# Two groups' transposes moved from TensorE to the DMA, and one pair of scores moved into the next tile, in a fused retention and feed-forward kernel

## The chip, the cores and the metric

The kernel runs on one core of a Trainium2 chip. The metric is the device time of one execution in microseconds (us); one profiled execution gives the trace. The span in the profile (first to last instruction) is about 2 us shorter than the device time. An execution of this one-core program is labelled slow when it is over 1.5% above the fastest of the same kernel; the text says where slow ones are quoted, and ratios use fast ones alone. The chip was not the same in every set of rounds (the record numbers them: e1 to e4 chip 2, f1 to f4 chip 1, h0 to h2 chip 6, i1 chip 5), so times are compared within a set.

## The reference

Eight batches of eight heads do retention (attention without softmax, with a decay by distance), and the result goes through a feed-forward layer whose nonlinearity is h·cos(h).

```python
scores = (1/sqrt(64)) * q @ k.T                  # q, k, v: (8, 8, 576, 64)
Dmat   = where(rel >= 0, gamma[h] ** rel, 0.0)   # rel = i - j
attn   = (scores * Dmat) @ v
x      = attn.transpose(0, 2, 1, 3).reshape(4608, 512)
h      = x @ w_in                                # (512, 2048)
out    = (h * cos(h)) @ w_out                    # (2048, 512), float32 out
```

## The kernel before

The 4608 tokens are 36 groups of 128. Each group's q and k are scaled (POOL), rounded to bf16 into `qks`, and transposed into `qkT`. Then come its scores (`sc`), its share of a running state (`st`) and its attention output (`ov`), which DVE or ACT copies into `xT`. Tiles of tokens (512, 256, 256, then seven of 512) go through `h = x @ w_in` (`mm1`, source line L275) and `o = g @ w_out` (`mm2`, L292). The small products of later groups are put between the products of `mm2` by a list `todo`: the number is the index of the `mm2` product in front of which the work goes. In words the first tile is tile n = 0, so "the fifth tile" is n = 4.

```python
widths = [512, 256, 256] + [512] * 7
N_PE_T = 8                       # groups below this are transposed on PE

def transposes(g, banks=None, only=(0, 1)):
    qks, vb, qkT, qT = tiles["a", g]
    if g >= N_PE_T:
        nc.sync.dma_start(qkT, qks.rearrange("s m h d -> s (m h d)"), transpose=True)
        return
    for m in only:               # 4 PE transposes and one ACT copy, for q and for k
        ...

def feed(s):                     # after output block s: issue loads and DMA transposes on SP
    while True:
        while prepared < min(loaded, NG, 2 * s + 7, s + 11):
            prep(prepared); prepared += 1
            ...
        if N_PE_T <= transposed < min(prepared, s + 11) and (
            transposed <= loaded - 2 or loaded == NG
        ):
            transposes(transposed); transposed += 1
        elif loaded < min(NG, 2 * s + 8, s + 13):
            load(loaded); loaded += 1
        else: break
...
elif n == 1:
    todo = [(4, lambda: transposes(6, "mb")), (9, lambda: transposes(7, "mb"))]
    todo += pair(6, "ab", 16, 27)
elif n == 2:
    todo = pair(g, "ab", 11, 25, "m")
    todo += [(25, lambda: scores2(g + 2)), (29, lambda: state(g + 2))]
    ...
```

All loads of q, k and v, output stores and DMA transposes are issued in program order by one engine, SP. A transpose late in that queue is late for its scores.

Of the kernel before, what the change touches and what calls it, by code (L numbers as in the profile page):

```python
# [17 lines left out]
def kernel(  # L18
# [16 lines left out]
    nc = tc.nc  # L35
# [8 lines left out]
    NG = NTOK // P  # L44
# [8 lines left out]
    widths = [512, 256, 256] + [512] * 7  # L53
    assert sum(widths) == NTOK
    starts = [sum(widths[:n]) for n in range(len(widths))]
    N_PE_T = 8

    consts = ctx.enter_context(tc.tile_pool(name="consts", bufs=1))
    first = ctx.enter_context(tc.tile_pool(name="first", bufs=1))
# [87 lines left out]
# [5 lines that stand above are left out]
        for m in only:  # L152
            ps = psum.tile([P, HG, P], BF16, tag=banks[m], name="tr")
            for hg in range(HG):
                nc.tensor.transpose(  # L155
                    ps[:, hg, :],
                    qks[:, m, 2 * hg : 2 * hg + 2, :].rearrange("s h d -> s (h d)"),
                    ident,
                )
            nc.scalar.copy(qkT[:, m * HG : (m + 1) * HG, :], ps)  # L160
        if ("fv", g) in tiles and g != 3:
            nc.scalar.copy(vb, tiles.pop(("fv", g)))
# [60 lines left out]
    def attn_out(gs, bank, evac=nc.vector.tensor_copy):  # L223


        ps = psum.tile([P, len(gs), HG, P], F32, tag=bank, name="ov")
        for x, g in enumerate(gs):
            c = g % PER
            if c == 0:
                continue  # L230
            qT = tiles["a", g][3]
            sb = tiles.pop(("sb", g))
            n = HP if c == MIX else P
            for hg in range(HG):
                nc.tensor.matmul(  # L235
                    ps[:, x, hg, :n],
                    lhsT=sb[:, hg, :],
                    rhs=qT[:, hg, :n],
                    start=(hg == 0),
                    stop=False,  # L240
                    skip_group_check=True,
                )
        for x, g in enumerate(gs):
            vb = tiles["a", g][1]
            ret = tiles.pop(("ret", g))
            for hg in range(HG):
                for he in range(2):
                    nc.tensor.matmul(  # L248
                        ps[he * D : he * D + D, x, hg, :],
                        lhsT=vb[:, 2 * hg + he, :],  # L250
                        rhs=ret[:, he, hg, :],
                        start=(g % PER == 0 and hg == 0),
                        stop=(hg == HG - 1),
                        skip_group_check=True,
                    )
        n = max(m for m in range(len(starts)) if starts[m] <= gs[0] * P)
        if ("x", n) not in tiles:
            tiles["x", n] = xp.tile([P, DG, 512], BF16, tag="xT", name="xT")
        t0 = gs[0] * P - starts[n]
        evac(  # L260
            tiles["x", n][:, :, t0 : t0 + len(gs) * P].rearrange("p c (x i) -> p x c i", i=P), ps
        )
# [45 lines left out]
    def feed(s):  # L308

        nonlocal loaded, prepared, transposed  # L310
        while True:
            while prepared < min(loaded, NG, 2 * s + 7, s + 11):
                prep(prepared)
                prepared += 1
                if transposed < N_PE_T:
                    transposed += 1

            if N_PE_T <= transposed < min(prepared, s + 11) and (
                transposed <= loaded - 2 or loaded == NG
# [114 lines left out]
    def pair(g, banks, sc, av, out=None):  # L434

        mid = (sc + av) // 2
        return [
            (sc - 5, lambda: state(g)),
            (sc, lambda: (scores(g, banks[0]), scores(g + 1, banks[1]))),
            (mid, lambda: state(g + 1)),  # L440
            (av, lambda: attn_out([g, g + 1], out or banks[0])),
        ]

    def scores2(g):
        if g < NG:
            scores(g, "a")
            scores(g + 1, "b")

    late = []
    for n, w in enumerate(widths):  # L450

        if n in (0, 3):
            halves = [(h, et) for et in range(0, ET, 4) for h in range(2)]
            if n == 3:
                halves.sort()
            blocks = [(et, half * 256, 256) for half, et in halves]
        elif n == 1:
            blocks = [(et, half * P, P) for half in range(2) for et in (0, 8)]
        else:
            blocks = [(et, 0, w) for et in range(0, ET, 1024 // w)]  # L460
        banks = {0: "abmabmab", 1: "bmba", 2: "bmab", 3: "mamabmab"}.get(n, "abmabmab")
        for i, (et, c0, cw) in enumerate(blocks):

            inside = {
                (0, 0): {2: lambda: (attn_out([3], "n"), state(3))},
                (1, 0): {4: lambda: scores(5, "a")},
                (1, 1): {3: lambda: attn_out([5], "a", evac=nc.scalar.copy)},
            }.get((n, i), {})
            mm1(n, et, c0, cw, banks[i], inside)
            if (n, i) == (3, 1):  # L470
                late.pop()()

        g = starts[n] // P + w // P
        if n == 0:
            todo = [
                (45, lambda: transposes(4, "ab")),
                (49, lambda: state(4)),
                (50, lambda: scores(4, "a")),
                (57, lambda: attn_out([4], "a")),
                (61, lambda: transposes(5, "ba")),  # L480
                (63, lambda: state(5)),
            ]
        elif n == 1:
            todo = [(4, lambda: transposes(6, "mb")), (9, lambda: transposes(7, "mb"))]
            todo += pair(6, "ab", 16, 27)
        elif n == 2:
            todo = pair(g, "ab", 11, 25, "m")
            todo += [(25, lambda: scores2(g + 2)), (29, lambda: state(g + 2))]
            late += [lambda: (state(g + 3), attn_out([g + 2, g + 3], "b"))]
        elif n + 1 < len(widths):  # L490
            todo = [
                (5, lambda: state(g)),
                (12, lambda: scores2(g)) if n == 3 else (0, lambda: None),
                (
                    25 if n == 3 else 20,
                    lambda: (
                        attn_out(
                            [g, g + 1], "m", nc.scalar.copy if n == 3 else nc.vector.tensor_copy
                        ),
                        scores2(g + 2),  # L500
                    ),
                ),
                (16, lambda: state(g + 1)),
                (36, lambda: state(g + 2)),
                (52, lambda: (attn_out([g + 2, g + 3], "m"), scores2(g + 4))),
                (45, lambda: state(g + 3)),
            ]
        else:
            todo = []
        todo.sort(key=lambda u: u[0])  # L510
        order, cols = [], [(0, DM)]
        for tsi in range(w // P):
            if (n + 1, tsi + 1) == (len(widths), w // P):
                cols = [(0, DM // 2), (DM // 2, 3 * DM // 4), (3 * DM // 4, DM)]
            order += [(tsi, et, c0, c1) for c0, c1 in cols for et in range(ET)]
        if n == 0:

            part = 3 * ET // 4
            order[: 2 * ET] = [
                (tsi, et, 0, DM)  # L520
                for tsi, et in [(t, e) for e in range(part) for t in range(2)]
                + [(t, e) for t in range(2) for e in range(part, ET)]
            ]
        for i, (tsi, et, c0, c1) in enumerate(order):
            while todo and todo[0][0] <= i:
                todo.pop(0)[1]()
            mm2(n, tsi, et, c0, c1)
        assert not todo
# [30 lines left out]
```

## Time and profile before

| | before |
|---|---|
| device time, median of the first 3 executions | 308.35 us (308.3 to 310.02) |
| span in the profile | 306.3 us |
| PE busy | 300.5 us (98%) |
| DVE, ACT, POOL busy | 57%, 38%, 32% |
| granted TensorE clock | 1.000 |

Lines of the page of the kernel before: span, busy time by engine, the span in 40 slices (7.66 us each; a digit is the busy share in tenths, PEclk the granted clock), and the chain of waits that ended last.

```profile
span 306.3 us, 5685 instructions
...
PE 300.5 (98%) x2361; PEld 171.2 (56%) x2361; DVE 175.8 (57%) x180; ACT 117.2 (38%) x136; POOL 99.0 (32%) x123
...
PE   7899999999999999999999999999999999999996
...
DMA  8999999999999999999993999189925300010012
...
PE 94%; SPq 2%; DMA 2%; DVE 0%; POOL 0%; issue 0%; ACT 0%; ACTq 0%
```

PE is the limit: after the first slices it is nearly never idle, and it is 94% of the chain. The DMA row is also 9 for the first half of the span: the SP queue runs behind its work there, and only what it delivers just in time matters.

PE's instructions of the kernel before in order of time. Columns: start us, duration, engine, line, operation, out<-in, shape, count, and in brackets idle time in front of it. A merged row's duration includes the last product's modelled end, so what counts is the distance between two starts.

```profile
58.33 0.61 PE L155 MATMUL tr<-ident,qks 128*128 128x128 bf16 x8
58.78 1.24 PE L292 MATMUL o<-w_out_sb,gT 128*128 128x512 bf16 x5
59.86 0.61 PE L155 MATMUL tr<-ident,qks 128*128 128x128 bf16 x8
60.30 0.59 PE L292 MATMUL o<-w_out_sb,gT 128*128 128x512 bf16 x2
...
60.96 1.24 PE L292 MATMUL o<-w_out_sb,gT 128*128 128x512 bf16 x5
...
66.41 1.25 PE L292 MATMUL o<-w_out_sb,gT 128*128 128x512 bf16 x5
67.79 7.15 PE L275 MATMUL h<-xT,w_in_sb 128*128 128x256 bf16 x64
...
81.94 0.62 PE L177 MATMUL sc<-qkT 64*128 64x128 bf16 x16
...
115.01 0.62 PE L177 MATMUL sc<-qkT 64*128 64x128 bf16 x16
```

Each lot of 8 transposes takes 0.45 us until the next product starts (58.33 to 58.78, 59.86 to 60.30). The five products at 66.41 need 5 × 0.216 = 1.08 us, so PE is free at 67.49, and the third tile's first product starts at 67.79: the hole of 0.3 us. The last row is the pair of scores (groups 16 and 17) that the change moves.

The SP queue of the kernel before, at group 8's and group 11's transposes (columns as above; the duration is the time that SP is held by the issue).

```profile
47.50 1.40 SPq L109 DMA_DIRECT2D fv<-in_v_dram  x1
49.00 1.05 SPq L303 DMA_DIRECT2D out_dram<-ot  x1
...
56.60 3.01 SPq L150 DMA_TRANSPOSE qkT<-qks  x1
...
74.17 2.02 SPq L150 DMA_TRANSPOSE qkT<-qks  x1
```

Group 11's transpose lands 5.0 us after its issue began, at 79.2 us. The 16 score products at 81.94 us are groups 10 and 11; group 11's half starts 0.28 us later, at 82.2, with 3.0 us of room.

### The profile page before, as it was taken

What the parts mean: (1) busy time and instruction counts of PE and PEld (TensorE: products, weight loads), DVE (VectorE), ACT (ScalarE), POOL (GpSimd) and SP (SyncE); (2) the same over time, 40 slices, a digit from 0 to 9 for tenths busy, and PEclk for the clock granted to TensorE, in tenths of its full rate; (3) what the DMA queues carried; (4) which work ended last, traced back from release to release, by engine and by line L of the source; (5) the groups of instructions that cost most, each with busy time, mean ns of one, the idle gap of its engine ahead of it and who ended that gap; (6) DMA issues with size and microseconds to landing.
All of it is one profiled execution on the core that took longest, in us unless ns stands there. A gap on an engine that the chain in (4) does not pass through costs nothing.

```text
span 306.3 us, 5685 instructions
## 1 busy us (share of the span) xinstructions
PE 300.5 (98%) x2361; PEld 171.2 (56%) x2361; DVE 175.8 (57%) x180; ACT 117.2 (38%) x136; POOL 99.0 (32%) x123
## 2 busy tenths in 40 slices
PE   7899999999999999999999999999999999999996
PEld 3478547757588554454545554455445544554444
DVE  5776425565777746656576556755676547624610
ACT  3566234715046223631264026411651165105611
POOL 2740066634554534544533334314430000000000
PEclk9999999999999999999999999999999999999999
DMA  8999999999999999999993999189925300010012
GB/s 210 213 211 206 205 230 229 190 198 246 164 243 208 196 253 199 268 220 205 258 205 58 223 218 225 23 190 208 243 48 77 99 35 0 36 68 34 2 68 69
DMA packets 148697, 49.65 MB, mean 162 GB/s; under 512 B 138688, under 2 KB 144192, under 8 KB 148672
## 3 DMA queue, kind: packets, MB, share of 16 engines
q1 hardware_dynamic: 144448, 45.10, 78.5%
q0 software_dynamic: 4224, 4.19, 8.2%
q8 instruction: 18, 0.29, 0.4%
q14 instruction: 7, 0.06, 0.1%
HBM read 36.70 MB, written 9.44 MB: 151 GB/s over the span
## 4 chain that ended last, share of the span: by engine, by line
PE 94%; SPq 2%; DMA 2%; DVE 0%; POOL 0%; issue 0%; ACT 0%; ACTq 0%
PE h L275 41%; PE o L292 41%; PE ov L248 3%; PE sc L177 3%; PE st L206 2%; PE ov L235 2%; DMA fk<-in_k_dram 2%; SPq L109 2%; PE tr L155 1%; PE sc L168 0%; DVE xT L260 0%; POOL qks L135 0%; SPq L336 0%; ACT ot L301 0%; ACTq L301 0%
## 5 line engine op out<-in xcount | busy, mean ns | idle before, releaser
L292 PE MATMUL o<-w_out_sb,gT 128*128 128x512 bf16 (+2 forms) x608 | 134.4, 369 | 0.0
L275 PE MATMUL h<-xT,w_in_sb 128*128 128x512 bf16 (+2 forms) x832 | 127.5, 314 | 0.1
L284 DVE TENSOR_TENSOR gT<-h,cosh 128x1024 bf16<-128x1024 f32 x72 | 88.2, 1225 | 55.9 <-ACT cosh L283 55.8
L275 PEld LDWEIGHTS <-w_in_sb 128*128 128x128 bf16 x832 | 75.8, 98 | 50.4 <-issue 0.4
L283 ACT ACTIVATE cosh<-h,half_pi 128x1024 f32<-128x1024 f32 x72 | 80.2, 1113 | 52.0 <-PE h L275 52.0
L292 PEld LDWEIGHTS <-gT 128*128 128x128 bf16 x608 | 55.3, 98 | 56.2
L134 POOL TENSOR_TENSOR qks<-fq,gq 128x512 bf16<-128x512 f32 x32 | 33.3, 1042 | 104.3 <-DMA fq<-in_q_dram 102.0
L301 ACT COPY ot<-o 128x512 f32<-128x512 f32 (+2 forms) x38 | 21.4, 563 | 115.4 <-PE o L292 115.4
L135 POOL TENSOR_TENSOR qks<-fk,gk 128x512 bf16<-128x512 f32 x35 | 36.5, 1042 | 13.1 <-DMA fk<-in_k_dram 11.4
L186 DVE TENSOR_TENSOR ret<-sc,tri 128x1024 bf16<-128x1024 f32 x32 | 38.0, 1218 | 4.6 <-PE sc L177 4.5
L215 DVE TENSOR_TENSOR sb<-st,diag_105 128x512 bf16<-128x512 f32 x32 | 22.0, 687 | 27.8 <-PE st L206 27.8
L260 DVE CAST xT<-ov 128x1024 bf16<-128x1024 f32 (+1 forms) x16 | 18.5, 1158 | 23.5 <-PE ov L248 23.5
L141 POOL CAST vb<-fv 128x512 bf16<-128x512 f32 x32 | 19.5, 610 | 7.7 <-DMA fv<-in_v_dram 5.7
L206 PEld LDWEIGHTS <-qks 128*128 128x128 bf16 (+1 forms) x128 | 9.5, 98 | 7.0 <-issue 0.4
L248 PE MATMUL ov<-ret,vb 128*64 128x128 bf16 x288 | 12.1, 223 | 0.0
L206 PE MATMUL st<-vb,qks 128*128 128x128 bf16 (+1 forms) x116 | 11.2, 220 | 0.1
L177 PEld LDWEIGHTS <-qkT 64*128 64x128 bf16 x288 | 8.1, 94 | 5.0 <-ACT qkT L160 2.3
L235 PEld LDWEIGHTS <-sb 128*128 128x128 bf16 x128 | 8.3, 98 | 3.8
L160 ACT COPY qkT<-tr 128x512 bf16<-128x512 bf16 x12 | 6.6, 588 | 9.3 <-PE tr L155 9.3
L177 PE MATMUL sc<-qkT 64*128 64x128 bf16 x256 | 10.1, 218 | 0.0
L248 PEld LDWEIGHTS <-vb 128*64 128x64 bf16 x288 | 8.7, 109 | 2.0
L235 PE MATMUL ov<-qkT,sb 128*128 128x128 bf16 (+1 forms) x116 | 8.8, 216 | 0.0
(49 smaller groups left out, 57.3 us busy)
## 6 DMA issues: line engine op xcount, KB each, us to landing
out_dram<-ot SPq DMA_DIRECT2D x35, 256.0 KB, 3.1
fk<-in_k_dram SPq DMA_DIRECT2D x32, 256.0 KB, 4.8
fv<-in_v_dram SPq DMA_DIRECT2D x32, 256.0 KB, 4.9
fq<-in_q_dram SPq DMA_DIRECT2D x28, 256.0 KB, 4.1
w_in_sb<-in_moe_w_in_dram POOLq DMA_DIRECT2D x4, 512.0 KB, 8.7
w_out_sb<-in_moe_w_out_dram POOLq DMA_DIRECT2D x4, 512.0 KB, 15.9
fq_111<-in_q_dram SPq DMA_DIRECT2D x2, 512.0 KB, 4.4
fq<-in_q_dram SPq DMA_DIRECT2D x8, 128.0 KB, 3.8
```

The costliest lines, as they stand in the source:

```text
L134: nc.gpsimd.tensor_tensor(out=qks[:, 0], in0=fq, in1=tq, op=ALU.mult)
L135: (nc.vector if g == 3 else nc.gpsimd).tensor_tensor(out=qks[:, 1], in0=fk, in1=tk, op=ALU.mult)
L177: nc.tensor.matmul(ps[:, he, hg, :], lhsT=qkT[d0 : d0 + D, HG + hg, :], rhs=qT[d0 : d0 + D, hg, :], start=True, stop=True,)
L186: nc.vector.tensor_tensor(out=ret.rearrange("p a b i -> p (a b) i"), in0=ps.rearrange("p a b i -> p (a b) i"), in1=mask.unsqueeze(1).to_br ...
L206: nc.tensor.matmul(ps[:, hg, :], lhsT=qks[p0:, 1, 2 * hg : 2 * hg + 2, :].rearrange("s h d -> s (h d)"), rhs=vs[p0:, 2 * hg : 2 * hg + 2, ...
L215: nc.vector.tensor_tensor(out=sb, in0=ps, in1=diag2.unsqueeze(1).to_broadcast([P, HG, P]), op=ALU.mult,)
L235: nc.tensor.matmul(ps[:, x, hg, :n], lhsT=sb[:, hg, :], rhs=qT[:, hg, :n], start=(hg == 0), stop=False, skip_group_check=True,)
L248: nc.tensor.matmul(ps[he * D : he * D + D, x, hg, :], lhsT=vb[:, 2 * hg + he, :], rhs=ret[:, he, hg, :], start=(g % PER == 0 and hg == 0), ...
L275: nc.tensor.matmul(ps[:, j, :], lhsT=w_in_sb[:, dg, (et + j) * P : (et + j + 1) * P], rhs=xT[:, dg, c0 : c0 + w], start=(dg == 0), stop=(d ...
L283: nc.scalar.activation(cosh, ps, ACTF.Sin, bias=half_pi, scale=1.0)
L284: nc.vector.tensor_mul(gT[:, et : et + m, c0 : c0 + w], ps, cosh)
L292: nc.tensor.matmul(ps, lhsT=gT[:, et, tsi * P : (tsi + 1) * P], rhs=w_out_sb[:, et, c0:c1], start=(et == 0), stop=(et == ET - 1),)
```

## The change

The intent is to take 16 transposes off PE, the limiting engine. Two more transposes in the DMA queue make every later one land later; group 17's was the tightest of those, so its scores, at the end of the fourth tile, move into the fifth. With them the fifth tile's first attention output goes from index 20 to 25, and its copy from DVE to ACT.

```diff
-    N_PE_T = 8
+    N_PE_T = 6
...
         elif n == 1:
-            todo = [(4, lambda: transposes(6, "mb")), (9, lambda: transposes(7, "mb"))]
-            todo += pair(6, "ab", 16, 27)
+            todo = pair(6, "ab", 16, 27)
...
-                (12, lambda: scores2(g)) if n == 3 else (0, lambda: None),
+                (12, lambda: scores2(g)) if n in (3, 4) else (0, lambda: None),
                 (
-                    25 if n == 3 else 20,
+                    25 if n in (3, 4) else 20,
                     lambda: (
-                        attn_out([g, g + 1], "m", nc.scalar.copy if n == 3 else ...),
+                        attn_out([g, g + 1], "m", nc.scalar.copy if n in (3, 4) else ...),
                         scores2(g + 2),
...
-                (52, lambda: (attn_out([g + 2, g + 3], "m"), scores2(g + 4))),
+                (
+                    52,
+                    lambda: (attn_out([g + 2, g + 3], "m"), scores2(g + 4 if n > 3 else NG)),
+                ),
```

## The prediction

> **What bounds the kernel now.** TensorE. The page's first part gives PE 300.5 of 306.3 us (98%) at full granted clock; the chain of waits is 94% PE, 41% each in the two big products. In order of time PE idles about 6 us, nearly all before 20 us; after that I find one hole, 0.3 us at 67.5 us, ended by DVE's xT copy. So only PE time removed, or PE waits added, count. ACT (38%), DVE (57%) and POOL (32%) have slack. The DMA is the second limit: its row is nearly always 9 until about 160 us, and the SP queue runs late there: the output that ACT copied at 49.2 us is issued at 70.9 us.
>
> **What the change removes.** Sixteen PE transposes. In PE's order of time two lots of 8 start at 58.33 and 59.86 us, each followed 0.45 us later by the next product: 0.9 us, all on the critical path. Four ACT copies of 0.59 us go too; with ACT's slack they are worth nothing.
>
> **What it adds.** Two DMA transposes on SP, one behind the loads of group 7 (about 49 us), one behind those of group 8 (about 55 us). Transposes issued there take SP 2.0 to 3.0 us and land 4.6 to 6.0 us after their issue begins. The Trainium skill, "Advanced Engine Details and Errata", section "X-Bar Transpose (TRN2)", says such transposes are as fast as regular DMAs; here a group's three loads take about 3.6 us of queue and an output 0.9, so the 17.6 us from group 8's transpose to group 11's leave about 1.7 us each (estimate), against a load's 1.2. So everything later in the queue moves by 3.4 us, less 0.4 to 1.2 us that SP now waits for POOL at group 8: 2.2 to 3 us, kept until the backlog ends near 159 us.
>
> **Who feels it.** Landing against use, before: group 11 lands at 79.2, its scores start at 82.2 (3.0 us spare, 2.1 once PE is 0.9 earlier); group 15: 101.9 against 107.3; group 17: 113.4 against 115.3, which would stall. That last the second part cures: those scores go to 12 products into the fifth tile, about 134 us. This follows the fourth tile's working pattern and adds no PE work. Group 7 should land near 60 us, its scores come at 61.5: just in time. Expected stalls, lost on PE: 0 to 0.9 us at group 11, 0 to 0.5 us at groups 6 and 7.
>
> **Prediction.** Gain 0.9 us, less about 0.3 expected stall: 307.7 us against 308.35. Range for 8 in 10: 307.0 to 308.7. Faster by over 2%: 0.01; within 2%: 0.98; slower by over 2%: 0.01.
>
> **What would show each step.** (a) No PE transposes after 50 us; the product at 60.96 us starts near 60.06. (b) Thirty DMA transposes, not 28; group 11's is issued 2 to 3 us later than 74.17. (c) The scores of groups 10 and 11 near 81.1 us, with a hole of 0 to 1 us before group 11's, ended by the DMA of qkT. (d) The fifth tile's first scores near 134 us, without a hole; later PE times early by the net gain. (e) The DMA's busy stretch ends 2 to 3 us later.
>
> **What would make it wrong.** A transpose that costs the full queue much more than 1.7 us: then groups 7, 11 and 15 stall and the change loses up to 2 us. A shift swallowed by holes in the DMA: then the whole 0.9 us is gained. New DVE or bank waits in the fifth tile.

## The result, and the profile after

The changed kernel took 307.93 us (median of 6 executions, 307.82 to 308.19), the kernel before 308.33 us (6 executions, 308.22 to 310.02). The ratio is 0.9979, with a 95% interval from 0.9958 to 1.0: the same within 2%, and about 0.4 us less. The interval reaches 1.0, so these times alone do not prove the gain; it is read from the traces below. (A ratio here is the mean time of one kernel's fast runs over that of the other's of the same rounds, so it is not quite the ratio of the medians.)

The page of the changed kernel.

```profile
span 305.9 us, 5619 instructions
...
PE 297.5 (97%) x2311; PEld 170.8 (56%) x2345; DVE 174.7 (57%) x179; ACT 116.1 (38%) x133; POOL 99.1 (32%) x123
...
PE 93%; SPq 2%; DMA 2%; issue 1%; DVE 0%; POOL 0%; ACT 0%; ACTq 0%
```

PE busy must not be read as a gain of 3 us: this trace misses some matmul records (582 instead of 608 of the `o` products), seen below as gaps of 0.16 us put down to "issue". Start times are the safer measure.

PE of the changed kernel in order of time, at the same places as before.

```profile
57.72 2.32 PE L292 MATMUL o<-w_out_sb,gT 128*128 128x512 bf16 x10
...
60.10 1.24 PE L292 MATMUL o<-w_out_sb,gT 128*128 128x512 bf16 x5
...
65.55 1.25 PE L292 MATMUL o<-w_out_sb,gT 128*128 128x512 bf16 x5
66.93 7.15 PE L275 MATMUL h<-xT,w_in_sb 128*128 128x256 bf16 x64
...
81.08 0.62 PE L177 MATMUL sc<-qkT 64*128 64x128 bf16 x16
...
131.87 1.67 PE L292 MATMUL o<-w_out_sb,gT 128*128 128x512 bf16 x7
133.47 0.62 PE L177 MATMUL sc<-qkT 64*128 64x128 bf16 x16
```

The transposes are gone. Every landmark up to 116 us is 0.86 us earlier: 60.96 to 60.10, 67.79 to 66.93, 81.94 to 81.08. No hole stands in front of group 11's scores. The hole at the third tile is still there (65.55 + 1.08 = 66.63, then 66.93). The moved scores are at 133.47; the seven products in front of them end at 131.87 + 7 × 0.216 = 133.38, so 0.09 us is lost between them.

The SP queue of the changed kernel.

```profile
48.02 1.34 SPq L109 DMA_DIRECT2D fv<-in_v_dram  x1
49.46 2.10 SPq L150 DMA_TRANSPOSE qkT<-qks  x1
...
54.56 3.10 SPq L150 DMA_TRANSPOSE qkT<-qks  x1
...
59.94 2.27 SPq L150 DMA_TRANSPOSE qkT<-qks  x1
...
75.94 2.05 SPq L150 DMA_TRANSPOSE qkT<-qks  x1
```

The rows are groups 6, 7, 8 and 11. Group 8's transpose is issued 3.34 us later than before (56.60 to 59.94). Group 11's transpose is issued 1.77 us later (74.17 to 75.94) and lands 5.2 us after that, at 81.14. Its scores start at 81.08 + 0.28 = 81.36. It made it by 0.2 us.

The end of both kernels: ACT's last copy of an output, in ACT's order of time, then SP's wait for output DMAs at the very end, in the table of waits (total us, times, longest us). First the kernel before, ACT and SP:

```profile
303.56 0.27 ACT L301 COPY ot<-o 128x128 f32<-128x128 f32 x1 [0.63 <-PE o L292]
```

```profile
SPq L554 <- DMA out_dram<-ot: 0.7, 1, 0.7
```

Then the changed kernel, ACT and SP:

```profile
302.81 0.27 ACT L301 COPY ot<-o 128x128 f32<-128x128 f32 x1 [0.63 <-PE o L292]
```

```profile
SPq L556 <- DMA out_dram<-ot: 1.1, 2, 0.8
```

PE's work, whose end ACT's last copy marks, finishes 0.75 us earlier (303.56 to 302.81), but the span is only 0.38 us shorter (306.33 to 305.95). The tail from the start of that copy to the end went from 2.77 to 3.14 us. The records of SP's wait instructions show why. At the end SP checks all DMA semaphores, in a fixed order, about 0.06 us per instruction (column 1: when the instruction started, us; then the semaphores it waits for):

```
before: last output issued at 303.86 on semaphore 118    changed: issued at 303.10 on semaphore 103
304.24  117, 116                                         303.48  117, 116
304.30  101, 115                                         303.83  101, 115
304.37  103, 114                                         304.68  103, 114   <- the last output has landed
304.44  104, 113                                         304.75  104, 113
304.50  105, 112                                         304.81  105, 112
304.56  106, 111                                         304.87  106, 111
304.62  108, 110                                         304.93  108, 110
304.68  109, 100                                         304.99  109, 100
305.43  118, 107   <- the last output has landed         305.05  118, 107
```

SP's DMAs take eight semaphores in turn (101, 103, 104, 105, 106, 108, 109, 118). Before, the last output happened to have the one that is checked last, so all the other checks were done while it was under way. Two more DMAs on SP turn this by two places: now it has the one checked third, and six checks come behind the landing: 305.05 − 304.68 = 0.37 us. So the account is: 0.86 us off PE, 0.11 back at the moved scores, 0.37 back in the tail, 0.38 us net.

### The profile page after: what moved, and what is told of

Its sections match the earlier page's. It is cut to its first block, busy times and chain, and to the rows that moved or that the text cites. A ratio compares the mean times of both kernels' runs of the same rounds, so it can differ in the third digit from the quotient of the medians.

```text
span 305.9 us, 5619 instructions
## 1 busy us (share of the span) xinstructions
PE 297.5 (97%) x2311; PEld 170.8 (56%) x2345; DVE 174.7 (57%) x179; ACT 116.1 (38%) x133; POOL 99.1 (32%) x123
## 4 chain that ended last, share of the span: by engine, by line
PE 93%; SPq 2%; DMA 2%; issue 1%; DVE 0%; POOL 0%; ACT 0%; ACTq 0%
PE h L275 41%; PE o L292 40%; PE ov L248 3%; PE sc L177 3%; PE ov L235 2%; PE st L206 2%; DMA fk<-in_k_dram 2%; SPq L109 2%; PE tr L155 0%; PE sc L168 0%; DVE xT L260 0%; POOL qks L135 0%; SPq L336 0%; ACT ot L301 0%; ACTq L301 0%
## 5 line engine op out<-in xcount | busy, mean ns | idle before, releaser
L292 PE MATMUL o<-w_out_sb,gT 128*128 128x512 bf16 (+2 forms) x582 | 130.3, 367 | 2.3 <-issue 1.6
L260 DVE CAST xT<-ov 128x1024 bf16<-128x1024 f32 (+1 forms) x15 | 17.3, 1153 | 20.9 <-PE ov L248 20.9
L160 ACT COPY qkT<-tr 128x512 bf16<-128x512 bf16 x8 | 4.5, 587 | 8.0 <-PE tr L155 8.0
```

What stands on the lines that cost most here:

```text
L292: nc.tensor.matmul(ps, lhsT=gT[:, et, tsi * P : (tsi + 1) * P], rhs=w_out_sb[:, et, c0:c1], start=(et == 0), stop=(et == ET - 1),)
```

## The experiments

Theory: the gain is PE's 0.86 us; the second part of the change is needed because group 17's transpose would otherwise come late, and costs 0.1 us; the rest is given back by the order of the semaphores. Rivals: the second part does nothing or helps by itself; the tail is a chance landing. Later runs ask why executions scatter, and try a better version. All twelve outputs were correct.

### e1: the first part alone

```diff
 # changed kernel, but:
-                (12, lambda: scores2(g)) if n in (3, 4) else (0, lambda: None),
+                (12, lambda: scores2(g)) if n == 3 else (0, lambda: None),
 # and scores2(g + 4) back at index 52 of the fourth tile;
 # the fifth tile's first attention output back at 20, with DVE's copy
```

> Both DMA transposes are kept, but the fifth tile's scores go back to the end of the fourth tile. Theory (the second part of the change cures a stall that the first part makes): the DMA transpose of group 17 lands near 115.0 us, as after the change, while its scores could start at about 114.4 us; PE has a hole of 0.4 to 0.8 us there, ended by that transpose, and the last ACT copy starts 0.3 to 0.7 us later than after the change (302.81 us). Rival (the second part is not needed, or only costs): no hole; the last ACT copy starts about 0.1 us earlier than after the change, near 302.7.

PE in order of time, at the end of the fourth tile:

```profile
114.22 0.40 PE L177 MATMUL sc<-qkT 64*128 64x128 bf16 x8
114.78 0.40 PE L177 MATMUL sc<-qkT 64*128 64x128 bf16 x8 [0.16 <-DMA qkT<-qks]
```

Group 17's scores start 0.56 us after group 16's, where 0.28 is usual: 0.28 us lost, ended by the DMA transpose, which landed at 114.73. The last copy is at 303.11, 0.30 us later than with the whole change. The sign and the releaser are as the theory said; the hole is smaller than the 0.4 to 0.8 us expected, because the transpose landed 0.3 us earlier than in the changed kernel's trace. Times: 308.2, 308.21, 308.74, 309.08, 309.2, 309.44 us, against a median of 308.35 before. In this trace the second part is worth 0.30 us; without it 0.45 us of the 0.75 us at the last copy is left (303.56 to 303.11).

### e2: the second part alone

```diff
 # changed kernel, but:
-    N_PE_T = 6
+    N_PE_T = 8          # and transposes(6), transposes(7) back in the list of n == 1
```

> The transposes of groups 6 and 7 stay on PE; only the fifth tile's scores move inside that tile. Theory (putting scores between two products of the tile costs a switch that scores behind an attention output don't have: 0.09 us between product and scores after the change): no DMA shift, no hole elsewhere, the last ACT copy starts 0.1 us later than before (303.56), so 303.65; the wall time is within 0.15 us of before. Rival (the move helps by itself, because the fifth tile's first product then finds free banks): the last ACT copy starts earlier than 303.56.

The last copy is at 303.72, 0.16 us later than before; the median is 308.45 against 308.35 us (all six between 308.42 and 308.47). It costs 0.1 to 0.16 us and has no gain of its own. The edit also moves one attention output and its copy, and their share of this was not separated. That scores behind a product lose 0.09 us, and scores behind an attention output lose nothing (81.37 + 16 products, then 81.94 directly in the kernel before), is read from the starts; why PE does so was not tested.

### e3 and e4: turning the semaphores

In e3 the changed kernel issues six more DMAs, in e4 the kernel before issues two more, by splitting output stores in halves at a time when SP is idle.

```diff
-            nc.sync.dma_start(out[s * P : (s + 1) * P, c0:c1], ot)
+            if 24 <= s < 30:                       # e4: 24 <= s < 26
+                for x0, x1 in ((0, 256), (256, 512)):
+                    nc.sync.dma_start(out[s * P : (s + 1) * P, x0:x1], ot[:, x0:x1])
+            else:
+                nc.sync.dma_start(out[s * P : (s + 1) * P, c0:c1], ot)
```

> The changed kernel with six output stores of the eighth tile and the one behind it split in two halves of the columns, so that SP issues six more DMAs at a time when it is idle. Theory (the end of the kernel waits for the DMA semaphores one pair after another, 0.06 us each; which semaphore the last output has goes round with the number of DMAs on SP, by eight; before it was the last in the order, after it is the third, and six more waits come behind its landing): the last output's semaphore is again the last in the order, the tail from the last ACT copy's start to the end is 2.77 us as before instead of 3.14, PE is unchanged (last copy at 302.8), and the wall time is about 307.55 us, 0.37 us under the changed kernel. Rival (the longer tail is a chance landing of the last output): tail near 3.1 us, 307.9 us or more.

> The kernel before with two output stores of the eighth tile split in halves: two more DMAs on SP, as the change adds two transposes. Theory of the order of the semaphores at the end: the tail becomes 3.14 us instead of 2.77, PE is unchanged, the wall time about 308.7 us, 0.37 us over before. Rival: unchanged, 308.33 us.

| | last output's semaphore | last copy | span | tail |
|---|---|---|---|---|
| before | 118, checked last | 303.56 | 306.33 | 2.77 |
| changed | 103, checked third | 302.81 | 305.95 | 3.14 |
| e3 | 118, checked last | 302.78 | 305.54 | 2.76 |
| e4 | 103, checked third | 303.62 | 306.84 | 3.22 |
| f4 (below) | 105, checked fifth | 308.94 | 312.00 | 3.06 |

Both tails turned as expected, in both directions, with PE unchanged, and f4's came out between (3.06 us, about 3.0 expected). The device times agree where executions were quiet: e4's median is 308.8 against 308.35 us, and e3's lowest is 307.47. But e3 scattered badly: 307.47, 307.75, 308.77, 308.83, 311.25 and a slow 312.86 us; its median showed nothing.

### f1 and f2: the changed kernel and e3 again

No edit: the changed kernel, and e3's kernel.

> The changed kernel once more, so that its runs share a chip and rounds with the two below, and because several executions of the last call were 0.5 to 2 us longer than others. Theory: PE's last copy near 302.8 us, tail 3.1 us, lowest wall time about 307.85 us, 0.4 us under before. If the transposes of groups 7 and 11 land only just in time (0.2 us of room at group 11), some executions are longer than that by some tenths of a us, and the runs of before are less spread.

> The same kernel as the one with six split stores, again, as its executions were too scattered in the last call (307.47 to 312.86 us). Theory of the order of the semaphores at the end: lowest and median wall time about 0.37 us under the changed kernel's of the same rounds, near 307.5 us. Rival: same as the changed kernel.

This was another chip than that of e1 to e4, and everything scattered on it. With the slow executions (before's 314.59, f1's 314.15, four of f2's six): before 308.16 to 314.59 us (median 308.75 of 11), changed 308.12 to 314.15 (median 309.8), f2 307.49 to 314.16. Medians settle nothing about the tail here; f2's lowest is again 0.6 us under f1's lowest. The gain of 0.4 us is not there in these rounds: f1's ratio to before is 1.0015 (interval 0.9972 to 1.0059). The traced execution of the changed kernel (309.84 us) shows a cause. PE in order of time:

```profile
80.98 0.40 PE L177 MATMUL sc<-qkT 64*128 64x128 bf16 x8
83.27 0.40 PE L177 MATMUL sc<-qkT 64*128 64x128 bf16 x8 [1.90 <-DMA qkT<-qks]
```

Group 11's transpose was issued at 77.03 and landed at 83.23 us, 2.1 us later than in the first trace; with 0.2 us of room, PE lost the other 1.9. This is the stall that the prediction had placed at group 11. Whether an execution has it depends on when the DMA lands in that execution. f2's traced execution, one of the slow ones (312.65 us), has it too. PE's wait in the table of waits:

```profile
PE sc L177 <- DMA qkT<-qks: 3.4, 1, 3.4
```

There group 11's transpose landed at 84.73 us, and the granted clock was one half from 85.90 to 89.31 us.

### f3: a first combination

The kernel of e3, with the attention output of groups 6 and 7 two products earlier, to close the hole at the third tile, and the scores of groups 10 and 11 two products later.

```diff
-            todo = pair(6, "ab", 16, 27)
+            todo = pair(6, "ab", 16, 25)
...
-            todo += [(25, lambda: scores2(g + 2)), (29, lambda: state(g + 2))]
+            todo += [(27, lambda: scores2(g + 2)), (29, lambda: state(g + 2))]
```

> A candidate that beats both: the changed kernel, the six split stores, the attention output of groups 6 and 7 two products earlier (25 instead of 27 in the second tile), and the scores of groups 10 and 11 two products later (27 instead of 25 in the third). Theory: the hole of 0.3 us in front of the third tile's first product, ended by the copy of xT, goes, so PE's last copy starts at about 302.5 us; group 11 has 0.6 us of room instead of 0.2; with the short tail (2.77 us) the span is about 305.25 and the wall time about 307.2 us, 1.1 us under before. Rival: the earlier attention output only moves the wait to another place, and the last copy stays at 302.8 us.

It missed: 308.1 to 312.12 us, where 307.2 was expected. Its shorter executions have no trace, so why even the fastest missed by 0.9 us stays open. The earlier attention output worked (the third tile's first product follows the product in front of it without a hole, at 66.79 us). Two products' delay was far too little for group 11. PE's wait for a DMA in the table of waits, then the clock row of the page, both of the traced execution (312.12 us):

```profile
PE sc L177 <- DMA qkT<-qks: 2.8, 1, 2.8
```

```profile
PEclk9999999999979999999999999999999999999999
```

Here a second cost shows. Behind the hole of 2.8 us the granted clock fell to one half for 3.41 us (85.04 to 88.45 us in the clock's records), which costs PE another 1.7 us (estimate: half of 3.41). The Trainium skill, "TensorE: Matmul & The Clock Gate", section "Why this matters for your kernels", advises no PE-idle gaps over about 3 us, because the clock then drops to half. This agrees, with a slightly lower threshold: holes of 1.77 (h0, below) and 1.90 us were not followed by half clock, holes of 2.81, 3.41 (f2) and 4.37 us (f4) were. The mean clocks of two long executions of the kernel before in these rounds, 0.994 (311.79 us) and 0.989 (314.59 us), are as low as f3's 0.994, so these too probably had stretches of half clock; they have no trace.

### f4: the two new transposes issued twice

The second copies go into a buffer that is dead by then.

```diff
             nc.sync.dma_start(qkT, qks.rearrange("s m h d -> s (m h d)"), transpose=True)
+            if g < 8:
+                again = qs4[:, 2 * g - 12 : 2 * g - 10]...   # nobody reads it
+                nc.sync.dma_start(again, qks.rearrange("s m h d -> s (m h d)"), transpose=True)
```

> The changed kernel with the two new DMA transposes issued twice, the second time into a tile that nobody reads. Theory (two such transposes push the DMA queue back by 1.8 us, which group 11 just survives with 0.2 us of room): two more push group 11's transpose another 1.5 to 2 us back, it lands near 82.8 us and PE has a hole of 1.2 to 1.8 us in front of group 11's scores, ended by that transpose; last copy near 304.2 us. With 32 transposes the last output's semaphore is the fifth in the order, the tail about 3.0 us. Rival (the queue has holes that swallow transposes): the shift is under 1 us and PE's hole under 0.6 us.

The table of waits, then the clock row of the page:

```profile
PE sc L181 <- DMA qkT<-qks: 4.4, 1, 4.4
```

```profile
PEclk9999999999979999999999999999999999999999
```

The hole is 4.37 us, over the 1.2 to 1.8 expected, as on this chip the hole was already there without the extra transposes (1.90 us in f1, 3.41 in f2). Group 11's transpose is issued at 79.80, against 77.03, 77.70 and 78.24 in the traces of f1, f2 and f3, which have the same transposes but for the extra two: 1.6 to 2.8 us later, or 0.8 to 1.4 us for each. On the first pair of traces it was 1.77 / 2 = 0.9. The rival (holes in the DMA swallow it, shift under 1 us) falls for these two. The second copies themselves hold SP for 1.23 and 1.25 us. The last copy is at 308.94, not at the 304.2 expected: the stall was longer, and the half clock was not foreseen. The clock halved again around the hole's end (85.77 to 89.18 us). In the traced execution 4.37 us of hole and about 1.7 us of half clock (3.41 us at one half) make 6.1 us, about what its span (312.0) is over the changed kernel's first (305.9). All four executions took 313.62 to 315.37 us; the ratio to before is 1.0172 (interval 1.0117 to 1.0227), by rule "unclear" at 2%, but slower.

### h0, h1: is group 11's deadline the scatter?

h0 is the changed kernel. h1 moves group 11's scores alone into the first product block of the fourth tile, 3.2 us later.

```diff
-            todo += [(25, lambda: scores2(g + 2)), (29, lambda: state(g + 2))]
+            todo += [(25, lambda: scores(g + 2, "a")), (29, lambda: state(g + 2))]
...
+                (3, 0): {3: lambda: scores(11, "b")},     # inside mm1 of tile n = 3
```

> The changed kernel, to be compared with the two below on the same chip. On a quiet chip about 307.9 us as at first; where the DMA is slower by a us or two, group 11's transpose comes late and executions are 1 to 3 us longer, and over 4 us longer where the hole gets so long that the granted clock halves behind it.

> The changed kernel with one thing moved: group 11's scores stand inside the first product block of the fourth tile, about 3 us later, no longer behind group 10's. Theory (the longer executions of the changed kernel come from the deadline of group 11's transpose): room of 3 us at group 11, no hole there; most executions near 308.0 us (0.1 us more than the changed kernel's best, for one more switch from products to scores), and the spread of its executions is clearly under the changed kernel's of the same rounds. Rival (the spread comes from elsewhere, other deadlines or the clock): the spread is as large as the changed kernel's.

PE of h1 around the moved scores:

```profile
83.16 1.47 PE L275 MATMUL h<-xT,w_in_sb 128*128 128x256 bf16 x12
84.57 0.40 PE L177 MATMUL sc<-qkT 64*128 64x128 bf16 x8
```

| same chip, same rounds | executions, us |
|---|---|
| before (11) | nine from 308.25 to 308.38, 308.4, 309.42 |
| h0, changed | 307.88, 307.94, 308.17, 309.32, 309.81, 311.46 |
| h1 | 308.0, 308.05, 308.09, 308.1, 308.12, 309.34 |

h0's traced execution (309.81) has the hole again, 1.77 us, ended by group 11's transpose. With the scores 3.2 us later, five of six executions lie within 0.12 us of each other; the sixth, 309.34, has no trace. In h1's own trace the transpose landed at 80.62 us, early enough for the old place too, so the evidence is in the spread. Over h1, h2 and i1 (below), which all have these scores later, 1 of 17 executions is over 308.5 us; over the changed kernel's three sets (the result, f1, h0) it is 8 of 18, the chips being partly others. That is good evidence for the theory, not a proof for every execution: f2's landing at 84.73 us would have been 0.16 us late even at h1's place. The kernel before scatters too, on f1's chip strongly; it has no trace of a long execution, so that cause stays open.

### h2: a candidate with more room everywhere

As h1, with e3's split stores, the earlier attention output of f3, group 15's scores 13 products later, and group 7's transpose in front of group 8's loads.

```diff
-                transposed <= loaded - 2 or loaded == NG
+                transposed <= loaded - (1 if transposed == 7 else 2) or loaded == NG
...
-                        scores2(g + 2),
+                        scores(g + 2, "a"),
+                        scores(g + 3, "b") if n > 3 else None,
...
+                (38, lambda: scores(g + 3, "b") if n == 3 else None),
```

> A candidate that beats both: group 11's scores as in the run above, group 15's scores 13 products later, group 7's DMA transpose issued in front of group 8's loads instead of behind them, the attention output of groups 6 and 7 two products earlier, and the six split stores that put the last output's semaphore last. Theory: no hole on PE after 20 us; last copy near 302.7 us (0.3 for the hole at the third tile, minus 0.2 for two more switches), tail 2.77 us, span 305.4, wall time 307.4 us, about 0.9 us under before, with little spread. Rival: the earlier transpose of group 7 or the later scores wait for something new, and the last copy is at 303 us or later.

It took 307.64, 307.65, 307.98, 308.35 and 308.48 us, median 307.98. PE had no hole, but the last copy was at 302.95, not 302.7: the extra switch to group 15's scores is the likely cost (not separated from the earlier transpose of group 7), and the room bought at groups 7 and 15 showed no benefit in this spread.

### i1: the candidate without those two

h1, the split stores, and the attention output at 25. Nothing else.

```diff
-            todo = pair(6, "ab", 16, 27)
+            todo = pair(6, "ab", 16, 25)
 # with h1's and e3's edits
```

> The candidate without what did not pay: group 11's scores inside the fourth tile's first product block, the attention output of groups 6 and 7 two products earlier, the six split stores; group 7's transpose and group 15's scores stay as in the changed kernel. Theory: against the run with the late scores of group 11 alone (last copy 303.03, tail 3.13 us, most executions 308.0 to 308.1), 0.29 us less for the hole at the third tile and 0.37 us less for the tail: last copy 302.75, span 305.5, most executions near 307.4 us, 0.9 us under before. Rival: the hole's 0.29 us comes back as a wait at another place (DVE or the banks), and executions stay at 307.7 us, as in the larger candidate.

PE at the third tile:

```profile
66.04 0.81 PE L292 MATMUL o<-w_out_sb,gT 128*128 128x512 bf16 x3
66.69 1.04 PE L275 MATMUL h<-xT,w_in_sb 128*128 128x256 bf16 x8
```

Three products need 0.65 us, so there is no hole (66.04 + 0.65 = 66.69). The last copy is at 302.78 (302.75 expected) and the span 305.54. Device times: 307.36, 307.39, 307.43, 307.46, 307.53, 307.93, median 307.45 against 308.35 us of before in the same rounds; the ratio is 0.9964 (interval 0.9946 to 0.9982). It beats the kernel before by 0.9 us and, across sets of rounds, the changed kernel by about 0.5 us.

## Why the prediction was right or wrong, point by point

The time was right: 307.93 us measured, 307.7 predicted, range 307.0 to 308.7. The net gain was smaller than predicted, 0.4 us against 0.65. It came out as near as that partly by luck: terms that were missed (0.11 and 0.37 us) stood in for a stall (0.3 us) that did not come in the traced execution.

- **What is removed.** Right: 0.9 us predicted, 0.86 us in every PE start from 60 to 116 us.
- **What a DMA transpose costs the queue.** About right in sum near the two transposes, by a doubtful split. Group 8's transpose is issued 3.34 us later, where two at 1.7 us make 3.4 (2.2 to 3 after the deduction). But the 1.7 us came from dividing up a stretch of queue time in which nine loads were put at 10.8 us: their issues hold SP for 8.2 us there, and 1.4 us of waiting for POOL and ACT, in SP's table of waits, was charged to the transposes. The cleaner measure is f4: its second copies hold SP for 1.23 and 1.25 us. This agrees with the Trainium skill's statement in "Advanced Engine Details and Errata", section "X-Bar Transpose (TRN2)", that such a transpose is as fast as a regular DMA: the prediction's figure for a load of the same 256 KB is 1.2 us of the queue.
- **The shift "kept until the backlog ends".** Wrong: it is 3.3 us at group 8, 1.8 at group 11, 1.4 at group 20 (126.09 to 127.50), 1.0 at group 25 (154.52 to 155.53). From group 8's issue to group 11's, the three transposes hold SP as long as before (7.5 us against 7.4), but the nine loads hold it for 6.5 us in place of 8.2; why was not tested. So part of the shift was swallowed, as "What would make it wrong" allowed, and this kept group 11 without a hole in the first trace: a shift of 3.34 us would have landed it near 82.6 us, 1.2 us after its place (estimate: 79.22 + 3.34 against 81.36). The forecasts of (b), 2 to 3 us at group 11, and of (e), 2 to 3 us at the end, failed with it.
- **Group 11 as the deadline in danger.** Right in kind. In the first trace it lands 0.2 us before its use, without a hole; in the traces of f1, h0 and f2 it is late and costs PE 1.9, 1.8 and 3.4 us. The prediction gave it at most 0.9 us and treated it as one number; it is a spread over executions.
- **Group 17 would stall without the second part.** Shown by e1, with 0.28 us.
- **The moved scores "add no PE work".** Wrong by 0.1 us: no work is added, but a switch from products to scores that they did not have behind an attention output (0.09 us in the trace, 0.16 us at the last copy in e2).
- **The end of the kernel.** Missing altogether: 0.37 us, shown by e3 and e4. It depends on the number of DMAs that SP issues, modulo eight.
- **Groups 6 and 7 just in time.** Group 7 landed at 60.16 us against 61.55, and no trace has a stall there.

## What to carry to other kernels

Work moved from a full engine into a DMA queue that runs behind costs nothing until a landing passes its deadline; so list each later landing against its use, and want room of more than the queue's variation between executions (up to 3.6 us here: 81.14 in the first trace, 84.73 in f2's), not just no hole in one trace. A single hole on PE can cost more than its length when the clock halves behind it. When a small gain on the limiting engine does not arrive in the time, compare the two ends too: here the number of DMAs alone decided 0.37 us of waiting.

## What the Trainium skill lacked or had wrong

- No page tells of the order in which the end of a kernel checks its DMA semaphores: 0.37 us between the third place and the last (e3, e4), turned by the number of DMAs on SP.
- "TensorE: Matmul & The Clock Gate", table of the two states: the clock is said to halve after at least one idle window of about 3.4 us. Here 2.81 us of idle PE was enough (f3), 1.90 us was not (f1); the half clock then lasted 3.41 us.
- "TensorE: Matmul & The Clock Gate", "Part 4: PE-mode transpose": it gives about 275 ns as the time of one 128×128 bf16 transpose in a kernel, and that section gives no distance from one to the next. In this trace one is shown with 0.22 us, but eight in a row take 0.45 us, 56 ns each, so 16 of them were worth 0.86 us; 16 times the page's figure, 4.4 us, would have been far off.
- No page read here gives the cost of scores put directly behind a product: 0.09 us per switch, and none behind an attention output.
- No page read here tells how far a full DMA queue varies: group 11's transpose landed at 81.14 us in one execution, at 83.23 in another (f1) and at 84.73 in a third (f2).
